# First loads of a fused attention and feed-forward block: q, k columns moved to another DMA queue, statistics of two tiles moved behind the first casts

## The chip, the cores and the metric

The kernel runs on one core of a Trainium2 chip. A core has five engines, each with its own instruction stream that runs in order: TensorE (PE, matrix products; its weight loads are listed as PEld), VectorE (DVE), ScalarE (ACT), GpSimd (POOL) and SyncE (SP), which here only starts transfers. Engines wait for each other through semaphores. Transfers are started by SP and by ScalarE, each with a queue of its own, and are carried out by 16 DMA engines. The metric is the device time of one execution in microseconds; lower is better.

## The reference

Inputs are in bf16: x is 1 x 2048 x 448, the hidden width of the feed-forward part is 1792.

```python
x = A_x
xn = _layernorm(x, axis=-1)
return x + _A_ref(xn, A_wqkv, A_wo) + _B_ref(xn, B_w_gate, B_w_up, B_w_down)

# _A_ref: 16 heads of 28, window of 256
qkv = (x @ wqkv).reshape(B, S, 3, H, Dh)           # then q, k, v
scores = einsum("bhqd,bhkd->bhqk", q, k) * Dh ** -0.5
mask = (i - j >= 0) & (i - j < 256)
o = einsum("bhqk,bhkd->bhqd", softmax(where(mask, scores, -1e9)), v)
return o.reshape(B, S, D) @ wo

# _B_ref
return (gelu(x @ w_gate) * (x @ w_up)) @ w_down
```

## The kernel before

The 2048 positions are 16 tiles of 128 and four blocks of 512. Everything is scheduled by hand: the order in which the Python code emits instructions is the order on each engine. A loop over the four blocks does attention and feed-forward of a block, and fills the time of the exponentials with matrix work of the neighbouring stages.

The part that the change touches comes before that loop and in its first steps.

Loads. SP starts x tile 0, x tiles 2 and 3, v's weights (rows 0 to 383, `wv`), the last 64 rows of q, k and v, x tiles 4 to 7, the remaining columns of q and k (`wraw`, L98), and then the first feed-forward weights. ScalarE starts x tile 1 and the first 4 heads' columns of q and k (L90).

Statistics. `stat(t)` (L155) takes mean and variance of tile t on DVE in two instructions (L157, L158). `rstd(t, n)` (L160) makes 1/sqrt(variance + 1e-5) from it, with a logarithm and an exponential on ACT (L166, L167), and for tile 5 alone with two instructions on POOL (L163, L164). `norm` (DVE, L176) or, for tile 1, `norm_scalar` (ACT, L184) applies it. For tiles 0 to 3 PE transposes the result (L199), and DVE or ACT copies it from PSUM to `xnT` (L200): DVE for tiles 0 and 3, ACT for 1 and 2. The transposes of tiles 0 and 2 use PSUM buffer b2, those of 1 and 3 use b3. Later tiles are transposed by DMA (`dma_transp`, L190).

First projections (L760 to L811). In PE's order: nine matmuls without use (`warmup`), transpose of tile 0, one more such matmul, transpose of tile 1, v of tile 0 (L776), transposes of tiles 2 and 3, v of tile 1, q and k of head group 0 (`proj`, L204), the last 64 rows of these (L210), v of tile 3. `pads` (L754) copies the q and k columns to a padded layout of 32 per head, first group 0 (q on DVE, k on ACT), then group 1, then 2 and 3. `qk_copies` casts q on ACT (L257) and k on DVE (L258) from PSUM; `v_copy` (L240) does so for v. On POOL, `make_masks` (L117) cuts the mask tiles, and `masked` (L619) applies the causal mask to the score blocks of steps 0 to 3, six instructions a step.

First block. For each step i of 8, scores are made on PE (L688), the exponential is taken on ACT (L693), and then the list `plan[i]` runs. `gen_qk` makes q and k of groups 1, 2 and 3 and is followed by `gen_up`, the up projection of the feed-forward part (L505, output `ue`). Their PSUM buffers are four (b0 to b3); `take` gives the one that has been free longest, `give` returns it at the end of the list. A group's q buffer is free once ACT has copied it, its k buffer once DVE has. The up projection's first pair uses the two buffers of group 2. `ahead2` (in `plan[1]`) takes statistics of tile 7 and normalises tiles 4 and 5, ahead of the cast of k of group 2; `ahead3` (in `plan[2]`) does tiles 6 and 7. The weighted sums of group 0 and 1 (`pv`, L662) come at steps 4 and 6 and read masked blocks of steps 0, 1 and 2, 3.

Of the kernel before, what the change touches and what calls it, by code (L numbers as in the profile page):

```python
# [16 lines left out]
S, D, H, Dh, F = 2048, 448, 16, 28, 1792  # L17
# [10 lines left out]
def kernel(  # L28
# [11 lines left out]
    nc = tc.nc  # L40
# [23 lines left out]
    wv = const.tile([P, 4, D], bf16, name="wv")  # L64
    v_sb = const.tile([P, NT, H, 32], bf16, name="v_sb")
    wraw = blk.tile([P, 4, 2 * D], bf16, name="wraw", tag="hT")
# [5 lines left out]
    def rows(w, c0, n):  # L72
        return w[c0 * P:(c0 + n) * P, :].rearrange("(c p) n -> p c n", p=P)
# [10 lines left out]
    wqk = rows(A_wqkv, 0, 3)[:, :, 0:2 * D]  # L84
    nc.sync.dma_start(out=x_sb[:, 0, :], in_=xv[:, 0, :])
    nc.vector.memset(x_sb[:, 1, 0:1], 0.0)
    nc.scalar.dma_start(out=x_sb[:, 1, :], in_=xv[:, 1, :])
    nc.sync.dma_start(out=x_sb[:, 2:4, :], in_=xv[:, 2:4, :])
    for c in (0, D):
        nc.scalar.dma_start(out=wraw[:, 0:3, c:c + 4 * Dh], in_=wqk[:, :, c:c + 4 * Dh])  # L90
    nc.sync.dma_start(out=wv[:, 0:3, :], in_=rows(A_wqkv, 0, 3)[:, :, 2 * D:3 * D])
    for a in range(2):
        nc.sync.dma_start(out=wraw[64 * a:64 * a + 64, 3, 0:D], in_=A_wqkv[384:448, a * D:(a + 1) * D])
    for a in range(2):
# [16 lines left out]
    def make_masks(n):  # L111
        for i, edges in list(enumerate(EDGES))[n]:
            for j, (_, *kinds) in enumerate(edges):
                for h, kind in enumerate(kinds):
                    if kind:
                        m = masks[64 * h:64 * h + 64, i, j, :]
                        nc.gpsimd.affine_select(out=m, in_=m, pattern=[[kind, 64]], compare_op=ALU.is_ge, fill=0.0,  # L117
                                                base=min(kind, 0), channel_multiplier=-kind)
# [36 lines left out]
    def stat(t):  # L155
        st = work.tile([P, nc.vector.BN_STATS_DIM], f32, name="st")
        nc.vector.bn_stats(out=st[:, :], in_=x_sb[:, t, :])  # L157
        nc.vector.bn_aggr(out=mv_all[:, t, :], in_=st[:, :])  # L158

    def rstd(t, n):  # L160
        lnv = work.tile([P, 4], f32, name="lnv")
        if t == 5:
            nc.gpsimd.tensor_scalar(out=lnv[:, 0:1], in0=mv_all[:, t:t + 1, 1], scalar1=1e-5, scalar2=None, op0=ALU.add)  # L163
            nc.gpsimd.tensor_tensor(out=rstd_all[:, t:t + 1], in0=lnv[:, 0:1], in1=minus_half[:, 0:1], op=ALU.pow)  # L164
            return
        nc.scalar.activation(out=lnv[:, 0:n], in_=mv_all[:, t:t + n, 1], func=ACT.Ln, bias=eps_t[:, 0:1], scale=1.0)  # L166
        nc.scalar.activation(out=rstd_all[:, t:t + n], in_=lnv[:, 0:n], func=ACT.Exp, scale=-0.5)  # L167
# [34 lines left out]
    def mm3(ps, lhs, rhs, start, stop):  # L202
        for c in range(3):
            nc.tensor.matmul(ps, lhsT=lhs(c), rhs=rhs(c), start=start and c == 0, stop=stop and c == 2,  # L204
                             skip_group_check=True)
# [27 lines left out]
    def v_dense(t, pv, first=True):  # L233
        mm3(pv, lambda c: xnT[:, c, t * P:(t + 1) * P], lambda c: wv[:, c, :], first, not first)
# [4 lines left out]
    def v_copy(t, pv, copy):  # L239
        copy(out=v_sb[:, t, :, 0:Dh], in_=pv.rearrange("p (h d) -> p h d", d=Dh))  # L240
        give(pv)
# [5 lines left out]
    def qk_halves(qb, g, pq, pk):  # L247
        w3 = w3p[:, 4 * g:4 * g + 4, :].rearrange("p h d -> p (h d)")
        for hi, ps in enumerate((pq, pk)):
            mm_half(ps, w3, xnT[:, 3, qb * QB:(qb + 1) * QB], hi, False, True)  # L250
# [73 lines left out]
    def deliver(qb):  # L324

        for j in range(4):
            nc.sync.dma_start(out=kT[32 * j:32 * j + Dh, 3, qb * QB:(qb + 1) * QB], in_=k3[j].rearrange("t i n -> (t i) n"))
# [149 lines left out]
    def new_hT(qb):  # L477
        hT = blk.tile([P, NF, QB], bf16, name="hT", tag="hT")
        hTs[qb] = hT
# [269 lines left out]
    def pads(eng, dst, gs):  # L749

        hs = slice(4 * gs.start, 4 * gs.stop)
        c0 = D * (dst is wkp)
        src = wraw[:, 0:3, c0 + Dh * hs.start:c0 + Dh * hs.stop]
        eng(out=dst[:, :, hs, 0:Dh], in_=src.rearrange("p c (h d) -> p c h d", d=Dh))  # L754
# [37 lines left out]
    nc.vector.tensor_copy(out=w3p[:, :, 0:Dh], in_=wraw[:, 3, 0:D].rearrange("p (h d) -> p h d", d=Dh))  # L792
    nc.vector.memset(masks[:, 0, 0, 0:1], 1.0)
    make_masks(slice(0, 1))
    stat(4)
    rstd(4, 1)
    stat(5)
    rstd(5, 1)
    make_masks(slice(1, 3))
    qk_halves(0, 0, pq, pk)  # L800
    for t in range(4):
        v_half(t, pvs[t], t < 2)
# [2 lines left out]
    v_copy(0, pvs[0], nc.scalar.copy)  # L805
    v_copy(1, pvs[1], nc.scalar.copy)
    pads(nc.vector.tensor_copy, wkp, slice(1, 2))
    v_dense(3, pvs[3], False)
    v_copy(3, pvs[3], nc.vector.tensor_copy)
    for dst in (wqp, wkp):  # L810
# [38 lines left out]
    for qb in range(NB):  # L849
        if qb in (1, 3):  # L850
            tc.mark_branch_hint_location("general", hint="LikelyTaken",
                                         engines=[mybir.EngineType.DVE if qb == 1 else mybir.EngineType.PE])
        early = ()
        if qb == 0:
            new_hT(0)
            early = (0, 1, 2, 3, 4)
            def last_v():
                v_dense(2, pvs[2], False)
                v_copy(2, pvs[2], nc.vector.tensor_copy)

            u = chain(gen_qk(), gen_up(0, (1, 2, 3, 0, 4), (2, 3, 4)))
            w = gen_pairs(1, (("v", 0), ("v", 2), ("k", 0), ("k", 1), ("k", 2)))
            plan = [[last_v, lambda: stat(6), (u, 3), ahead], [(u, 2), ahead2, (u, 2)], [(u, 1), ahead3, (u, 7)], [(u, 8), lambda: stat(8)],
                    [lambda: stat(9), (u, 12), lambda: fill_pads(True)], [(u, 9), "sums"],
                    [(w, 7), "inverse", "scale", (w, 7), lambda: stat(10), (w, 3)],
                    [(w, 4), lambda: stat(11), lambda: rstd(8, 4), (w, 7), "masks", "sums", (w, 7), "inverse"]]
        else:
            d = gen_down(qb - 1)
            if qb < 3:
                u = gen_pairs(qb + 1, (("v", 0), ("k", 0), ("v", 2), ("k", 1), ("k", 2)))  # L870
                plan = [[(d, 14)], [(d, 11)], [(d, 11)], [(u, 7)], [(d, 17)], ["sums", (d, 1), (u, 7), "inverse"], [(u, 11)],
                        [lambda: q_last(qb + 1, nc.vector.tensor_copy), (d, 6), "sums"], [(d, 2), "inverse", (d, 9)],
                        [(u, 9), "masks", (u, 1)]]
                plan[3] = [(d, 1), (u, 7)]
                if qb == 2:
                    plan[0], plan[2] = [(d, 13)], [(d, 10)]
                if qb == 1:
                    for i, j in enumerate((0, 1, 2, 2)):
                        plan[j].insert(0, lambda t=12 + i: stat(t))
                    plan[4].append(lambda: rstd(12, 4))  # L880
                    plan[1] = plan[1][:1] + [lambda: q_last(1, nc.vector.tensor_copy), (d, 8)]
                    plan[2] = plan[2][:2] + [(d, 12), lambda: collect(1)]
                    plan[4].append(lambda: deliver(1))
            else:
                new_hT(3)
                early = (1, 2, 3, 4, 5, 6)
                u = gen_up(3, early, (4, 5, 6))
                plan = [[(u, 12)], [(u, 9)], [(d, 12)], [(d, 10)], [(d, 12)], [(d, 1), (u, 7), "sums"], [(d, 12), "inverse"],
                        ["sums", "inverse", (d, 11)], [(d, 11)], [(d, 1), "masks", (u, 13), "masks", (u, 1)]]
        if qb in (1, 2):  # L890
            swap(qb + 1)
        score_pool(1)
        rest, after, flush = attention(qb, plan)
        nc.scalar.preload_act_table(ACT.Gelu_apprx_tanh)
        score_pool(2)
        if qb not in hTs:
            new_hT(qb)

        def hook(f):
            after(f)  # L900
            if qb in (1, 2) and f == 0:
                collect(qb + 1)
            if f == (8, 2, 2, 0)[qb]:
                o_collect(qb)
            if f == (12, 4, 4, 0)[qb]:
                o_deliver(qb)
                o_finish(qb)
            if qb == 0 and f == 10:
                nc.gpsimd.tensor_copy(out=wo[64:128, 3, :], in_=wo[0:64, 3, :])
            if qb in (1, 2) and f == 10:  # L910
                deliver(qb + 1)
            t = ({0: 8, 4: 9, 8: 10, 10: 11} if qb == 0 else {4: 12, 6: 13, 8: 14, 10: 15} if qb == 1 else {}).get(f)
            if t is not None:
                norm(t)
                dma_transp(t)
            if qb == 0 and f == 4:
                load_wo(3, 4)

        gated(qb, early, rest, flush, hook)
        if qb < NB - 1:  # L920
            nc.scalar.preload_act_table_set("natural_log_exp_and_others")
# [159 lines left out]
```

## Time and profile before

| | us |
|---|---|
| median of 3 runs | 211.65 (211.53 to 212.1) |
| span of the profiled execution | 210.4 |
| first matrix product that is part of the result (v of tile 0) | starts at 7.34 |
| last addition (L402) | 207.50 to 207.90 |

The profiled execution's span is from its first to its last instruction; the time of a run has some 1.25 us more around it (211.65 less 210.4). Times in the views are from the start of the span. A row of the timeline gives start, duration, engine and line, operation, output and inputs with their shapes, and how often; in brackets stands the idle time of the engine before it and what ended that. SPq and ACTq rows are the issues of transfers, not the transfers. The chain of work that ended last is short in this profile (the last addition and what follows it), so the path is read from the timeline of each engine.

### The profile page before, as it was taken

To read this page: it belongs to the slowest core of one execution; us is meant where nothing else is said; L and a number is where in the kernel's file an instruction comes from. 1 tells how busy PE (TensorE), PEld (TensorE's weight loads), DVE (VectorE), ACT (ScalarE), POOL (GpSimd) and SP (SyncE) were. 2 spreads that over 40 slices of the span, in tenths; PEclk is the share of its full clock that TensorE was granted. 3 is DMA by queue.
4 is the path that set the end of the run, shared out by engine and by line. 5 is a ranking of instruction groups with operands and counts; after the bars stand their busy time and mean duration, and the time that the engine had idled before them with its cause. 6 is when DMAs were issued, how large, how long until landed. Compare 5 with 4: busy or idle time off the path is not lost. (4 is left out here: it accounts for less than half of the span.)

```text
span 210.4 us, 6677 instructions
## 1 busy us (share of the span) xinstructions
PE 205.3 (98%) x2842; PEld 98.4 (47%) x2842; DVE 156.6 (74%) x360; ACT 134.5 (64%) x132; POOL 44.3 (21%) x89
## 2 busy tenths in 40 slices
PE   7899999999999999999999999999999999999994
PEld 2443444544454545444445444544444454544572
DVE  6798989899788985696438897395385699596532
ACT  4689896956677977413778788523587787756000
POOL 5289932241000220040000112013000022032000
PEclk9999999999999999999999999999999999999999
DMA  5999599973341001003331000100000010100011
GB/s 171 277 244 207 112 207 224 296 237 82 74 103 53 25 11 31 9 3 72 71 75 47 25 3 24 23 3 21 22 5 0 3 47 3 45 9 16 3 47 50
DMA packets 24890, 15.68 MB, mean 75 GB/s; under 512 B 9208, under 2 KB 24728, under 8 KB 24856
## 3 DMA queue, kind: packets, MB, share of 16 engines
q1 hardware_dynamic: 23912, 14.93, 30.2%
q8 instruction: 23, 0.38, 0.7%
q10 hardware_dynamic: 944, 0.29, 0.6%
q14 instruction: 11, 0.09, 0.2%
HBM read 9.26 MB, written 2.41 MB: 55 GB/s over the span
## 5 line engine op out<-in xcount | busy, mean ns | idle before, releaser
L693 ACT ACTIVATE p_sb<-sc 128x2048 bf16<-128x2048 f32 x38 | 71.4, 1879 | 16.9 <-PE sc L688 11.7
L545 ACT ACTIVATE p_sb<-gt 128x1024 bf16<-128x1024 f32 x28 | 28.6, 1025 | 31.3 <-PE gt L505 30.4
L628 POOL TENSOR_TENSOR oN<-oc,l 128x512 bf16<-128x512 f32 x16 | 20.7, 1298 | 120.5 <-DVE l L641 120.5
L505 PE MATMUL gt<-xnT,wg 64*128 64x512 bf16 x224 | 45.6, 376 | 0.0
L414 PE MATMUL po<-wd,hT 128*128 128x448 bf16 (+1 forms) x224 | 44.7, 347 | 0.0
L505 PE MATMUL gt<-xsw,wg 64*128 64x512 bf16 x168 | 40.7, 376 | 0.0
L613 DVE TENSOR_TENSOR p_sb<-p_sb,masks 128x256 bf16<-128x256 bf16 (+1 forms) x98 | 30.9, 369 | 7.4 <-ACT p_sb L693 7.4
L555 DVE TENSOR_TENSOR hT<-p_sb,u 128x512 bf16<-128x512 bf16 x34 | 21.8, 675 | 13.5 <-PE u L505 13.5
L414 PEld LDWEIGHTS <-hT 128*128 128x128 bf16 x238 | 21.9, 98 | 19.1 <-issue 2.2
L505 PEld LDWEIGHTS <-wg 64*128 64x128 bf16 x392 | 19.0, 94 | 22.3
L505 PEld LDWEIGHTS <-wu 64*128 64x128 bf16 x392 | 18.7, 94 | 22.2 <-issue 0.4
L505 PE MATMUL u<-xnT,wu 64*128 64x512 bf16 x136 | 28.1, 376 | 0.0
L505 PE MATMUL u<-xsw,wu 64*128 64x512 bf16 x102 | 24.7, 376 | 0.0
L505 PE MATMUL ue<-xnT,wu 64*128 64x512 bf16 x88 | 18.0, 377 | 0.0
L647 DVE TENSOR_TENSOR oc<-oc,ov 128x512 f32<-128x512 f32 (+1 forms) x16 | 10.4, 656 | 10.0 <-ACT oc L645 9.9
L505 PE MATMUL ue<-xsw,wu 64*128 64x512 bf16 x66 | 16.3, 377 | 0.0
L688 PE MATMUL sc<-qT,kT 28*64 28x320 bf16 (+4 forms) x736 | 16.2, 259 | 0.0
L402 DVE TENSOR_TENSOR res<-po,x_sb 128x448 bf16<-128x448 f32 (+1 forms) x14 | 8.1, 605 | 7.8 <-PE po L414 6.7
L688 PEld LDWEIGHTS <-kT 28*64 28x64 bf16 x736 | 8.1, 103 | 12.3 <-issue 11.0
L522 DVE CAST hT<-ue 128x512 bf16<-128x512 f32 x16 | 10.5, 685 | 2.7 <-PE ue L505 2.7
L645 ACT COPY oc<-ov 128x512 f32<-128x512 f32 x16 | 9.3, 585 | 4.0 <-PE ov L662 4.0
L641 DVE STREAM_TRANSPOSE l<-inv_all 128x512 f32<-128x512 f32 x16 | 11.1, 701 | 0.1
(115 smaller groups left out, 257.0 us busy)
## 6 DMA issues: line engine op xcount, KB each, us to landing
out_dram<-res SPq DMA_DIRECT2D x15, 112.0 KB
wd<-in_B_w_down_dram SPq DMA_DIRECT2D x2, 784.0 KB
x_sb<-in_A_x_dram SPq DMA_DIRECT2D x3, 448.0 KB
xsw<-xnT SPq DMA_DIRECT2D x6, 192.0 KB
wg<-in_B_w_gate_dram SPq DMA_DIRECT2D x2, 560.0 KB
wu<-in_B_w_up_dram SPq DMA_DIRECT2D x4, 224.0 KB
wu<-in_B_w_up_dram SPq DMA_DIRECT2D x2, 336.0 KB
wraw<-in_A_wqkv_dram SPq DMA_DIRECT2D x2, 252.0 KB
```

The source lines that it names most:

```text
L414: nc.tensor.matmul(po[:, 0:w], lhsT=x[:, k, tt * P:(tt + 1) * P], rhs=wt[:, k, lo:up], start=start and n == 0, stop=stop and n == len(term ...
L505: nc.tensor.matmul(ps, lhsT=w[64 * hi:64 * hi + 64, c, p * P:(p + 1) * P], rhs=xchunk(qb, hi, c, qb * QB, QB), start=c == 0, stop=c == 6, ...
L522: copy(out=hTs[qb][:, p + 7 * i, :], in_=us[i])
L545: nc.scalar.activation(out=ges[p][:, :, :], in_=gt[:, :, :], func=ACT.Gelu_apprx_tanh)
L555: nc.vector.tensor_tensor(out=hT[:, p + 7 * i, :], in0=ge[:, i, :], in1=u, op=ALU.mult)
L613: nc.vector.tensor_tensor(out=reg, in0=reg, in1=m, op=ALU.mult)
L628: nc.gpsimd.tensor_tensor(out=oN[:, g, :], in0=oc[:, :], in1=inv, op=ALU.mult)
L641: nc.vector.transpose(out=l1[:, :, :], in_=inv_all[:, 4 * qb + g, :].unsqueeze(2).to_broadcast([P, 16, 32]))
L645: nc.scalar.copy(out=oc[:, :], in_=ov[0][:, :])
L647: nc.vector.tensor_tensor(out=oc[:, q0:], in0=oc[:, q0:], in1=ov[1][:, q0:], op=ALU.add)
L688: nc.tensor.matmul(ss[k0:k0 + nk, j, col:col + nq], lhsT=kT[r, g, kt * P + k0:kt * P + k0 + nk], rhs=qT[r, g, ring(qb).start + q0:ring(qb) ...
L693: nc.scalar.activation(out=p_sb[:, :, 0:ncol], in_=ss[:, :, 0:ncol], func=ACT.Exp, scale=SCALE)
```

## The change

Three parts. The loads of the first 4 heads' q and k columns go from ScalarE's queue to SP's, behind the load of v's weights; ScalarE's queue keeps x tile 1 alone. The statistics of tiles 4 and 5, tile 5's rstd on POOL and the second and third mask tiles go from ahead of the last rows of q, k of group 0 to behind the casts of group 0 and the padded copies of group 1. Tile 4's rstd on ACT goes into the plan of the first attention step.

```diff
     nc.scalar.dma_start(out=x_sb[:, 1, :], in_=xv[:, 1, :])
     nc.sync.dma_start(out=x_sb[:, 2:4, :], in_=xv[:, 2:4, :])
+    nc.sync.dma_start(out=wv[:, 0:3, :], in_=rows(A_wqkv, 0, 3)[:, :, 2 * D:3 * D])
     for c in (0, D):
-        nc.scalar.dma_start(out=wraw[:, 0:3, c:c + 4 * Dh], in_=wqk[:, :, c:c + 4 * Dh])
-    nc.sync.dma_start(out=wv[:, 0:3, :], in_=rows(A_wqkv, 0, 3)[:, :, 2 * D:3 * D])
+        nc.sync.dma_start(out=wraw[:, 0:3, c:c + 4 * Dh], in_=wqk[:, :, c:c + 4 * Dh])
     for a in range(2):
...
     make_masks(slice(0, 1))
-    stat(4)
-    rstd(4, 1)
-    stat(5)
-    rstd(5, 1)
-    make_masks(slice(1, 3))
     qk_halves(0, 0, pq, pk)
     for t in range(4):
         v_half(t, pvs[t], t < 2)
     qk_copies(0, 0, pq, pk)
     pads(nc.vector.tensor_copy, wqp, slice(1, 2))
     v_copy(0, pvs[0], nc.scalar.copy)
     v_copy(1, pvs[1], nc.scalar.copy)
     pads(nc.vector.tensor_copy, wkp, slice(1, 2))
+    stat(4)
+    stat(5)
+    rstd(5, 1)
+    make_masks(slice(1, 3))
     v_dense(3, pvs[3], False)
     v_copy(3, pvs[3], nc.vector.tensor_copy)
...
-            plan = [[last_v, lambda: stat(6), (u, 3), ahead], [(u, 2), ahead2, (u, 2)], [(u, 1), ahead3, (u, 7)], [(u, 8), lambda: stat(8)],
+            plan = [[last_v, lambda: rstd(4, 1), lambda: stat(6), (u, 3), ahead], [(u, 2), ahead2, (u, 2)], [(u, 1), ahead3, (u, 7)], [(u, 8), lambda: stat(8)],
```

## The prediction

> **What bounds the kernel now.** I read the page first, then busy time in stretches of 5 us.
>
> ```profile
> span 210.4 us, 6677 instructions
> ...
> PE 205.3 (98%) x2842; PEld 98.4 (47%) x2842; DVE 156.6 (74%) x360; ACT 134.5 (64%) x132; POOL 44.3 (21%) x89
> ```
> ```profile
> 10.00:15.00 5.00, 5.00 (x64) 1.88 (x63) 4.69 (x13) 4.27 (x7) 4.14 (x17) 1.00 1.09 248
> 15.00:20.00 5.00, 5.00 (x52) 1.84 (x58) 4.97 (x13) 4.97 (x7) 4.66 (x14) 1.00 1.21 240
> ```
>
> In the second fence each row gives the stretch, its length, then busy us and instructions of PE, PEld, DVE, ACT and POOL, the granted clock and the DMA share. PE has no idle left from 10 us on; the end is where PE's stream starts plus its length. So the change is worth what it moves that stream, early on, less any new hole in it. VectorE (DVE) and ScalarE (ACT) are full too between 15 and 20 us: 4.97 of 5. That stretch has no room for more work. The clock is 1.00 throughout.
>
> The hole at the start, in the timeline of PE alone (start, duration, instruction, idle time before it):
>
> ```profile
> 6.30 0.40 PE L199 MATMUL tp<-ident,xn 128*128 128x128 bf16 x4
> 7.34 0.73 PE L204 MATMUL pv<-wv,xnT 128*128 128x448 bf16 x3 [0.65 <-DMA wv<-in_A_wqkv_dram]
> 7.91 0.61 PE L199 MATMUL tp<-ident,xn 128*128 128x128 bf16 x8
> ```
>
> PE waits 0.65 us for v's weights. Everything behind stands in line: the transposes of x tiles 2 and 3, then the projections.
>
> **The loads.** In the DMA view of 3.2 to 7.3 us (packets, MB, share of 16 engines) SP's queue is q1, and ScalarE's, q10, holds only the first q, k columns:
>
> ```profile
> q1 hardware_dynamic: 1110, 0.91, 76.6%
> q10 hardware_dynamic: 800, 0.17, 20.4%
> ```
> ```profile
> 1.48 0.99 ACTq L90 DMA_DIRECT2D wraw<-in_A_wqkv_dram  x2
> ```
>
> They take 20.4% of 4.1 us = 0.84 us of each engine, in the very time in which v's weights travel. Behind them on one queue they leave that 0.84 to the weights: landing 7.34 - 0.84 = 6.50. The bounds: no gain at all (7.34), or all of it. I take nearly all, since the packets of the two queues stand in the same stretch.
>
> A rule of the Trainium skill, page "DMA: Bandwidth & Descriptors", section "Issuing engines are not separate DMA queues", speaks against this: transfers from any engine run on the same 16 engines and interleave, and a second issuer saves only its issue time. Read strictly it makes the move worth nothing and the time 212.6; that is rival 2. The 20.4% above counts against it, since order within a queue is what changes.
>
> SP issues two more DMAs, 0.99 us by ACT's row. Its later loads, tiles 4 to 7 among them, are issued that much later, but the engines are still at work on what was issued before, so landing follows the bytes, which are the same. SP also waits for these columns, in its timeline:
>
> ```profile
> 5.78 2.08 SPq L98 DMA_DIRECT2D wraw<-in_A_wqkv_dram  x2
> ```
>
> The two issues of the remaining q, k columns, some 0.4 us of work each, are stretched over 2.08 us because each waits until the first columns of its half have landed, the k half at about 7.5. Landing of the k columns at 6.50 + 0.84 = 7.34 leaves that as it is. On ACT 0.99 us of issue time goes, before an activation that waits for DVE's statistics anyway: worth nothing.
>
> **How much earlier PE gets.** The views of DVE and of ACT (one row):
>
> ```profile
> 6.19 0.39 DVE L200 COPY xnT<-tp 128x512 bf16<-128x512 bf16 x1
> 6.70 0.81 DVE L176 TENSOR_SCALAR xn<-x_sb,mv_all,rstd_all 128x448 bf16<-128x448 bf16 x2
> 7.43 0.27 DVE L754 COPY wqp<-wraw 128x336 bf16<-128x336 bf16 x1
> 8.55 0.42 DVE L200 COPY xnT<-tp 128x512 bf16<-128x512 bf16 x1 [0.86 <-PE tp L199]
> ...
> 9.21 0.63 DVE L157 BATCH_NORM_STATS2 st<-x_sb 128x6 f32<-128x448 bf16 x1
> ...
> 10.60 0.18 DVE L158 BATCH_NORM_AGGREGATE mv_all<-st 128x2 f32<-128x6 f32 x1
> 10.90 0.69 DVE L258 CAST kT<-s 128x512 bf16<-128x512 f32 x1
> ...
> 11.69 0.26 DVE L754 COPY wkp<-wraw 128x336 bf16<-128x336 bf16 x1
> 11.92 0.62 DVE L240 CAST v_sb<-pv 128x448 bf16<-128x448 f32 x1
> ...
> 14.29 0.18 DVE L158 BATCH_NORM_AGGREGATE mv_all<-st 128x2 f32<-128x6 f32 x1
> 14.59 0.69 DVE L258 CAST kT<-pk 128x512 bf16<-128x512 f32 x1
> ...
> 17.45 0.68 DVE L258 CAST kT<-pk 128x512 bf16<-128x512 f32 x1
> ...
> 19.43 0.68 DVE L258 CAST kT<-pk 128x512 bf16<-128x512 f32 x1
> 20.70 0.69 DVE L522 CAST hT<-ue 128x512 bf16<-128x512 f32 x1 [0.59 <-PE ue L505]
> ```
> ```profile
> 6.99 0.57 ACT L200 COPY xnT<-tp 128x512 bf16<-128x512 bf16 x1
> ```
>
> Tile 0's activations are copied at 6.58, so the first v projection could start at 6.65. The transposes of tile 3 follow in PE's order, but they write the PSUM buffer that ACT's copy of tile 1 frees at 6.99 + 0.57 = 7.56, whatever the loads do. Four transposes take 0.40 (row of 6.30): tile 3's copy starts at 7.56 + 0.05 + 0.40 = 8.01 in place of 8.55. So the head gains at most 0.53, call it d, and all up to the first casts (L257, L258) moves with it. DVE must have copied the first q columns by 8.01, so they must land by 7.74; half of 0.84 behind 6.50 puts them at 6.92. If in one line they went at the pace of the other packets (q1: 76.6% of 4.1 us on 16 engines for 1110 packets, 45 ns each; 24 packets per engine) they would land at 7.58: still in time. I take d = 0.45, some hand-offs below the bound; d runs from 0 to 0.53.
>
> **The statistics.** The pair of tiles 4 and 5 costs DVE 10.60 + 0.18 - 9.21 = 1.57 us, about 1.5 as instructions overlap a little at their ends. Today it lies in front of the cast at 10.90, which waits for PE and not for DVE (free at 10.78). With PE earlier by d it would stand in the way; so it goes behind the casts. But what it leaves is a hole in DVE from about 8.7 to 10.4, and where it goes DVE is full: from 10.90 to 20.1 it has only one wait, at 14.59 for PE (it was free at 14.47, and could have begun at about 14.40: 0.17). So every DVE instruction behind it comes at -d + 1.5, from the cast of group 1 at -d + 1.33.
>
> Who waits for that? PSUM buffers pass round. Of the q, k buffers of group 2, the first that the feed-forward's up projection takes needs ACT's copy, the second the cast of 17.45 to 18.13. PE takes them here:
>
> ```profile
> 18.53 0.38 PE L505 MATMUL ue<-xsw,wu 64*128 64x512 bf16 x1
> ```
>
> Slack today: 18.53 - 18.13 - 0.05 = 0.35. Ahead, the buffers of the v copies and the padded weights of groups 2 and 3 have slack of 0.2 or more by the same sum and hold. So PE stops there until 18.13 + 1.33 - d + 0.05, and goes on later than today by 1.33 - 0.35 - d = 0.98 - d. With d = 0.45: **+0.53 us**. Behind it PE is again the slower one (DVE's 0.59 of idle time at 20.70), so the delay stays to the end; nothing later gives it back, since PE is full.
>
> GpSimd (POOL) says the same by another road. Tile 5's rstd (L163) stands in its order ahead of the masks and the masked score blocks:
>
> ```profile
> 11.49 0.31 POOL L163 TENSOR_SCALAR lnv<-mv_all 128x1 f32<-128x1 f32 x1
> ...
> 24.58 2.64 POOL L619 TENSOR_SCALAR_AFFINE_SELECT p_sb<-p_sb 64x256 bf16<-64x256 bf16 x6
> ```
> ```profile
> 28.11 0.62 PE L662 MATMUL ov<-p_sb,v_sb 64*32 64x320 bf16 x36
> ```
>
> It now waits for the statistics, 11.92 - 0.45 + 1.57 + 0.05 = 13.09, 1.6 later. POOL has no wait from there to 27.2, so the last masked block ends at 27.22 + 1.6 = 28.8. The weighted sum of group 1 uses that block in its second half, from about 28.35 today: +0.5 as well. Two roads to the same size make the lag more likely, and removing one alone would not remove it.
>
> The rstd of tile 4 moves on ACT behind the first exponential:
>
> ```profile
> 16.81 0.30 ACT L166 ACTIVATE lnv<-mv_all,eps_t 128x2 f32<-128x2 f32 x1
> 17.14 0.20 ACT L167 ACTIVATE rstd_all<-lnv 128x2 f32<-128x2 f32 x1
> ```
>
> Its 0.50 us delays the copy of q of group 1, by some 0.2 net, and the second exponential by as much; PE meanwhile has d in hand, so at most 0.1 shows, inside the lag above and not added to it. Without that cover it would cost up to 0.5.
>
> **Sum.** Span 210.4 + 0.53 = 210.9; the median of the runs, 211.65, lies 1.25 above the span, so 212.2.
>
> **Rivals.** 1, the forecast: 212.2, from 211.9 (d = 0.53 and a lag 0.15 shorter) to 212.6; chance 0.63. 2, v's weights land no earlier: d = 0, 0.98 of lag: 212.6. For it: the engines are near full, and the skew between them may set the landing. Against: the 20.4%. Chance 0.13. 3, not slower: DVE's lag does not reach PE and d stays to the end: 211.65 - 0.5 = 211.15. It decides at the up projection's second matmul: the group 2 cast must end by 18.53 - d - 0.05, and POOL's last block must not bind, so both lags must shrink by about 1 us. For it: only my reading of the buffers' round and of two queues' order says otherwise. Against: two full engines. Chance 0.14. 4, the first q columns come late in one line: each 0.1 after 7.74 takes 0.1 from d. With both halves at 45 ns ahead of DVE's copy, 6.50 + 2.16 = 8.66, tile 3's copy starts at 8.93, d = -0.4: 211.65 + 1.4 = 213.0. For it: such short packets (0.17 MB in 800) are not seen in one line with the others. Against: the 0.8 us to spare at the pace that q10 shows. Chance 0.10.
>
> **Numbers.** A measurement here can tell about 0.3% = 0.63 us from no change: above 212.28 or below 211.02. Slower: half of rival 1, and 2 and 4: 0.53. Faster: the better part of rival 3: 0.09. Within: 0.38. Range 211.3 to 212.9: it reaches rival 2 whole, most of 4 and up to 3.
>
> **What would show it.** Right: the first v matmul at about 6.7 with no DMA wait, tile 3's copy at about 8.05, DVE idle up to 10.4, the cast of group 2 ending near 19.0, an idle stretch of about 1 us on PE at the up projection with DVE as releaser, POOL's L163 near 13.1. Wrong: the first v matmul still at 7.3 (rival 2), no PE idle near 18 to 19 (rival 3), DVE waiting for wraw at the first padded copy (rival 4).

## The result and the profile after

| | before | after |
|---|---|---|
| median of 13 runs each, same chip, us | 211.65 (211.45 to 212.74) | 213.05 (212.61 to 215.05) |
| ratio, with 95% interval | | 1.0068 (1.0049 to 1.0088) |
| span of the profiled execution | 210.4 | 211.1 |

The change makes the kernel slower by 1.4 us; 212.2 was forecast, with a range that ended at 212.9. The page of the profile after, and its busy time by stretch (us from the start, length, then busy us and instructions of PE, PEld, DVE, ACT and POOL, granted clock, DMA share, GB/s):

```profile
span 211.1 us, 6677 instructions
...
PE 205.2 (97%) x2842; PEld 98.1 (46%) x2842; DVE 155.9 (74%) x360; ACT 134.4 (64%) x132; POOL 43.9 (21%) x89
```
```profile
5.50:8.00 2.50, 1.79 (x17) 1.15 (x18) 2.00 (x7) 2.35 (x7) 0.00 (x0) 1.00 0.54 126
...
15.00:20.00 5.00, 4.55 (x42) 1.59 (x39) 4.93 (x14) 4.32 (x6) 4.44 (x16) 1.00 1.17 255
```

PE does the same work in the same time. Between 15 and 20 us it now has 0.45 us of idle time where it had none, and between 5.5 and 8 us the DMA engines are half idle. The same stretch of before:

```profile
5.50:8.00 2.50, 1.85 (x14) 0.92 (x13) 2.03 (x7) 1.99 (x6) 0.00 (x0) 1.00 1.00 271
```

PE's timeline of after, at the three places that count (start, duration, engine and line, operation, count, and in brackets the idle time before it):

```profile
6.55 0.74 PE L204 MATMUL pv<-wv,xnT 128*128 128x448 bf16 x3
...
18.01 0.37 PE L505 MATMUL ue<-xnT,wu 64*128 64x512 bf16 x1
18.83 0.39 PE L505 MATMUL ue<-xsw,wu 64*128 64x512 bf16 x2 [0.45 <-DVE kT L258]
...
28.41 0.54 PE L662 MATMUL ov<-p_sb,v_sb 64*32 64x320 bf16 x20
29.11 0.35 PE L662 MATMUL ov<-p_sb,v_sb 64*32 64x320 bf16 x16 [0.17 <-POOL p_sb L619]
```

The wait for v's weights is gone (6.55 against 7.34). At the up projection PE stands still for the cast of group 2 and is 0.30 late (18.83 against 18.53). At the weighted sum of group 1 it waits for POOL's masked block: the two halves of that sum were 28.11 and 28.35 before, 0.24 apart; now they are 0.70 apart, and the second is 0.76 late. The span ends 0.72 later. So these two places, 0.30 at the first and 0.46 (0.70 less 0.24) at the second, account for the difference between the two profiles. DVE and POOL in their timelines:

```profile
7.34 0.27 DVE L754 COPY wqp<-wraw 128x336 bf16<-128x336 bf16 x1
7.94 0.42 DVE L200 COPY xnT<-tp 128x512 bf16<-128x512 bf16 x1 [0.33 <-PE tp L199]
...
10.28 0.69 DVE L258 CAST kT<-s 128x512 bf16<-128x512 f32 x1 [1.72 <-PE s L210]
10.89 0.27 DVE L754 COPY wqp<-wraw 128x336 bf16<-128x336 bf16 x1
11.47 0.28 DVE L754 COPY wkp<-wraw 128x336 bf16<-128x336 bf16 x1 [0.32 <-DMA wraw<-in_A_wqkv_dram]
11.66 0.61 DVE L157 BATCH_NORM_STATS2 st<-x_sb 128x6 f32<-128x448 bf16 x1
...
16.84 1.36 DVE L176 TENSOR_SCALAR xn<-x_sb,mv_all,rstd_all 128x448 bf16<-128x448 bf16 x4
18.10 0.68 DVE L258 CAST kT<-pk 128x512 bf16<-128x512 f32 x1
```
```profile
13.38 0.23 POOL L163 TENSOR_SCALAR lnv<-mv_all 128x1 f32<-128x1 f32 x1 [2.59 <-DVE mv_all L158]
...
26.70 2.36 POOL L619 TENSOR_SCALAR_AFFINE_SELECT p_sb<-p_sb 64x256 bf16<-64x256 bf16 x6
```

DVE is idle for 1.72 us ahead of its cast at 10.28: the hole that the statistics left. Then comes a wait that the forecast did not have: 0.32 us for the remaining k columns, straight ahead of the statistics. POOL waits 2.59 us for these and ends its last masked block at 26.70 + 2.36 = 29.06, just before PE's second half starts.

SP's queue after, and what its small loads weigh (KB each in the DMA view):

```profile
2.23 1.02 SPq L91 DMA_DIRECT2D wraw<-in_A_wqkv_dram  x2
3.29 1.21 SPq L93 DMA_DIRECT2D wraw<-in_A_wqkv_dram  x2
4.55 1.24 SPq L95 DMA_DIRECT2D wv<-in_A_wqkv_dram  x2
5.83 0.58 SPq L96 DMA_DIRECT2D x_sb<-in_A_x_dram  x1
6.46 1.04 SPq L98 DMA_DIRECT2D wraw<-in_A_wqkv_dram  x2
```
```profile
wraw<-in_A_wqkv_dram SPq DMA_DIRECT2D x2, 56.0 KB
wv<-in_A_wqkv_dram SPq DMA_DIRECT2D x2, 56.0 KB
```

The four loads of last rows (L93, L95) cost SP some 0.6 us each to issue and carry 56 KB, which at 271 GB/s is 0.21 us. From 3.29 to 5.79 SP issues only these. What lay ahead of them is used up by about 5.5, and tiles 4 to 7 (L96) and the remaining columns (L98) are issued only then. The events of these loads' semaphores in the traces agree: tiles 4 to 7 have landed at 9.58, at 9.18 before, and the remaining k columns at 11.44, at 10.74 before. With two issues less ahead of it on this queue, the issue of tiles 4 to 7 stood 1.06 us earlier before the change:

```profile
4.77 0.59 SPq L96 DMA_DIRECT2D x_sb<-in_A_x_dram  x1
```

### The profile page after: what moved, and what is told of

Read it like the earlier page. It is cut to its first block, busy times and chain, and to the rows that moved or that the text cites. A ratio compares the mean times of both kernels' runs of the same rounds, so it can differ in the third digit from the quotient of the medians.

```text
span 211.1 us, 6677 instructions
## 1 busy us (share of the span) xinstructions
PE 205.2 (97%) x2842; PEld 98.1 (46%) x2842; DVE 155.9 (74%) x360; ACT 134.4 (64%) x132; POOL 43.9 (21%) x89
## 5 line engine op out<-in xcount | busy, mean ns | idle before, releaser
L613 DVE TENSOR_TENSOR p_sb<-p_sb,masks 128x256 bf16<-128x256 bf16 (+1 forms) x98 | 30.4, 364 | 7.6 <-ACT p_sb L693 7.6
L662 PE MATMUL ov<-p_sb,v_sb 64*32 64x320 bf16 (+4 forms) x720 | 11.0, 253 | 0.2 <-POOL p_sb L619 0.2
```

What stands on the lines that cost most here:

```text
L613: nc.vector.tensor_tensor(out=reg, in0=reg, in1=m, op=ALU.mult)
L662: nc.tensor.matmul(ov[half][32 * j:32 * j + 32, q0:q0 + nq], lhsT=v_sb[r, kt, 4 * g + j, :], rhs=p_sb[r, j, col:col + nq], start=n == half ...
```

## The experiments

Two questions: which part costs what, and by which road; and why the measured 1.4 is more than the 0.53 of the forecast. The theory: the moved statistics cost by DVE and by POOL, the moved loads cost because SP's later loads come late, and the first profile of before was of an execution slower than its median. The rivals: that one part alone makes all of the loss; that POOL's road or DVE's alone is the bound; that the 1.25 us around the span holds. Ratios are against runs of the kernel before that were taken together with each (medians 211.68 to 211.81).

**The kernel before, again.** No edit.

> The kernel before, unchanged, for more executions and a second profile. Theory A (the profile that the forecast rests on was a slow execution, 0.4 us above the median run): spans of the median run near 209.95 us, so that run time less span is about 1.7 us and not 1.25; first v matmul of this profile at 6.7 to 7.1 us instead of 7.34. Rival B (the moved loads themselves cost more than was counted): the profile looks as the first one did, v at 7.3, span 210.4 at a median of 211.65.

211.68, ratio 0.9998 (0.9989 to 1.0007). Its profiled execution has a span of 210.1 in a run of 211.80, 1.7 apart, and so are run and span in the other runs, to within 0.2 (for the profiled one of after: 212.79 and 211.1). A median of 211.65 goes with a span near 209.95, and the profile that the prediction rests on was 0.4 above that. In PE's timeline the hole is smaller: v's first matmul starts 0.25 earlier than in the first profile, and the span ends 0.28 earlier (210.08 for 210.36). The row names a DVE instruction that ended just then, but the load of v's weights has landed only at 7.05 by its semaphore:

```profile
6.28 0.40 PE L199 MATMUL tp<-ident,xn 128*128 128x128 bf16 x4 [0.23 <-ACT xn L184]
7.09 0.73 PE L204 MATMUL pv<-wv,xnT 128*128 128x448 bf16 x3 [0.42 <-DVE xn L176]
```

**The loads alone.**

```diff
+    nc.sync.dma_start(out=wv[:, 0:3, :], in_=rows(A_wqkv, 0, 3)[:, :, 2 * D:3 * D])
     for c in (0, D):
-        nc.scalar.dma_start(out=wraw[:, 0:3, c:c + 4 * Dh], in_=wqk[:, :, c:c + 4 * Dh])
-    nc.sync.dma_start(out=wv[:, 0:3, :], in_=rows(A_wqkv, 0, 3)[:, :, 2 * D:3 * D])
+        nc.sync.dma_start(out=wraw[:, 0:3, c:c + 4 * Dh], in_=wqk[:, :, c:c + 4 * Dh])
```

> Only the loads move; the statistics of tiles 4 and 5 stay ahead of the first casts. These wait for tiles 4 to 7, which landed at about 9.6 us in the changed kernel, so the cast of k is not before 11.15 us (10.90 before). Theory A: 0 to +0.5 us against before (211.6 to 212.1). Rival B: the later landing of everything on SP's queue is most of the 1.4 us: +1.0 us or more (212.6).

212.21, ratio 1.0018 (1.0009 to 1.0027): the loads alone cost 0.5 by the medians, 0.4 by the ratio. DVE in the timeline:

```profile
9.79 0.63 DVE L157 BATCH_NORM_STATS2 st<-x_sb 128x6 f32<-128x448 bf16 x1 [1.17 <-DMA x_sb<-in_A_x_dram]
...
11.28 0.66 DVE L258 CAST kT<-s 128x512 bf16<-128x512 f32 x1
```

v's first matmul is at 6.62, but tile 4 is not there when DVE wants it (its load lands at 9.77 by its semaphore), and the statistics hold up the cast of group 0, 0.64 behind its 10.64 in the second profile of before. With the loads moved and the statistics left in place, it is these that wait for x.

**The statistics alone.** `stat(4)`, `stat(5)`, `rstd(5, 1)` and the masks behind the first casts and tile 4's rstd in the plan as in the change, the loads as before.

> Only the statistics move; the loads stay as before. Theory A with the forecast's sum at d = 0: +1.0 us (212.6), PE idle at the up projection's second matmul and again at the weighted sum of group 1 (waiting for POOL). Rival B: at most +0.4 us (212.0).

212.70 (212.56 to 213.01), ratio 1.0043 (1.003 to 1.0056): +1.0. In POOL's and PE's timelines of this kernel:

```profile
13.27 0.23 POOL L163 TENSOR_SCALAR lnv<-mv_all 128x1 f32<-128x1 f32 x1 [2.32 <-DVE mv_all L158]
```
```profile
28.54 0.53 PE L662 MATMUL ov<-p_sb,v_sb 64*32 64x320 bf16 x20
29.33 0.34 PE L662 MATMUL ov<-p_sb,v_sb 64*32 64x320 bf16 x16 [0.26 <-POOL p_sb L619]
```

POOL waits as in the kernel after, and PE waits for it. The wait at the up projection that was expected is not marked in this profile: its second matmul is at 18.45, 0.18 behind the 18.27 of the second profile of before. So here POOL's road sets the end almost alone. This is the larger part of the loss, and the moved loads have no share in it.

**POOL's road taken away, with the loads moved.**

```diff
     stat(4)
     stat(5)
+    make_masks(slice(1, 3))
     rstd(5, 1)
-    make_masks(slice(1, 3))
```

> The changed kernel with the second and third mask tiles ahead of tile 5's rstd on POOL, so that POOL works while it waited 2.6 us. If POOL's road sets the end (0.73 us late at the weighted sum of group 1, 0.30 at the up projection): 0.4 us less than the changed kernel, 212.6, and no wait for POOL at the weighted sum. If DVE's road alone sets it: no difference, 213.05.

212.44, ratio 1.0042 (1.0025 to 1.0059): 0.6 less than the kernel after. POOL's row, then PE's:

```profile
14.22 0.23 POOL L163 TENSOR_SCALAR lnv<-mv_all 128x1 f32<-128x1 f32 x1
```
```profile
18.73 0.39 PE L505 MATMUL ue<-xsw,wu 64*128 64x512 bf16 x2 [0.41 <-DVE kT L258]
```

POOL has no wait left, since it makes the masks while DVE does the statistics; PE still stops at the up projection. Each road costs by itself. How the 0.6 is made up is less sure: the k columns landed at 11.23 in this profile and DVE copied them at 11.25, 0.22 earlier than in the kernel after, though the loads are the same.

**The same, with the loads as before.**

> Loads as before, statistics behind the first casts, the mask tiles ahead of tile 5's rstd on POOL: DVE's road alone. Two roads (theory): POOL's part, 0.6 us, falls away from the 1.0 us of the kernel with the statistics alone: 212.05 to 212.2, PE idle only at the up projection. If POOL's wait was all of it: 211.7, as before.

212.43, ratio 1.0037 (1.0024 to 1.005): DVE's road alone costs 0.7, more than was expected here. The up projection's second matmul is at 18.77, 0.50 behind the 18.27 of the second profile of before.

**The loads moved, x tiles 4 to 7 issued sooner; the statistics as before.**

```diff
+    nc.sync.dma_start(out=x_sb[:, 4:8, :], in_=xv[:, 4:8, :])
     for a in range(2):
         nc.sync.dma_start(out=wraw[64 * a:64 * a + 64, 3, 0:D], in_=A_wqkv[384:448, a * D:(a + 1) * D])
     for a in range(2):
         nc.sync.dma_start(out=wv[64 * a:64 * a + 64, 3, :], in_=A_wqkv[384:448, 2 * D:3 * D])
-    nc.sync.dma_start(out=x_sb[:, 4:8, :], in_=xv[:, 4:8, :])
```

> Loads moved, statistics ahead of the casts as before, and x tiles 4 to 7 issued ahead of the last 64 rows of q, k and v. If the 0.45 us that the loads alone cost come from SP's issues, which bring tiles 4 to 7 0.6 us later and hold the statistics up, this removes them: tiles land by 9.0, cast of k at 10.4 to 10.5, 0.1 to 0.3 us faster than before (211.4 to 211.6). If the late columns or rows of q and k cost it: 212.0 or more.

211.76, ratio 1.0001 (0.9992 to 1.001): the 0.5 of the loads is gone. In the busy time by stretch and in SP's timeline:

```profile
5.50:8.00 2.50, 2.12 (x21) 1.19 (x19) 2.06 (x7) 2.34 (x7) 0.00 (x0) 1.00 1.01 271
```
```profile
3.30 0.49 SPq L92 DMA_DIRECT2D x_sb<-in_A_x_dram  x1
```

The issues are as many as in the kernel after, on the same queue and for the same bytes, but one of 448 KB now stands ahead of the four small ones, and the engines are full: 271 GB/s in place of 126. Tiles 4 to 7 have landed at 8.20 in place of 9.77. So it was the order that starved the engines: small loads at 0.6 us an issue with nothing large behind which to hide. There is no gain over before, though v's first matmul is at 6.67: now the last rows of q, k come late (DVE waited 0.20 for them at 8.68), and the cast of k, expected at 10.4 to 10.5, is at 10.79.

**One pair ahead, one behind.** `stat(4)` stays ahead of group 0's last rows, `stat(5)`, the masks and then `rstd(5, 1)` go behind, in the order of the kernel with POOL's road taken away; loads as in the change.

> Changed loads and their order, mask tiles first on POOL, statistics of tile 4 ahead of the casts and of tile 5 behind. DVE's lag shrinks by 0.75 us, below what PE has to spare, so no idle PE at the up projection: 211.5 to 211.8. If the lag is set by something else than the inserted statistics: 212.4, as with the mask tiles first alone.

211.98, ratio 1.0017 (1.0007 to 1.0028), somewhat above what was expected. DVE's row:

```profile
9.97 0.63 DVE L157 BATCH_NORM_STATS2 st<-x_sb 128x6 f32<-128x448 bf16 x1 [1.12 <-DMA x_sb<-in_A_x_dram]
```

The pair ahead waits 1.12 us for x, so the place is free but what it needs isn't there.

**The split, and tiles 4 to 7 sooner.**

> Loads moved, tiles 4 to 7 ahead of the last rows, mask tiles first on POOL, statistics of tile 4 ahead of the casts and of tile 5 behind. If late tiles and late q, k columns were what kept the split of the statistics from paying (cast of k at 10.73 instead of 10.3, 0.34 us of DVE waiting for the columns): cast of k at 10.3 to 10.4, cast of group 2 done by 17.9, no idle PE at the up projection, its second matmul at about 18.0, span 209.8, time 211.4 to 211.5. If DVE is still the bound there: 211.8 or more.

211.60 (211.41 to 212.23), ratio 1.0001 (0.9992 to 1.0011). In PE's timeline there is no wait left at the up projection:

```profile
17.93 0.38 PE L505 MATMUL ue<-xnT,wu 64*128 64x512 bf16 x1
17.93 0.59 PE L505 MATMUL ue<-xsw,wu 64*128 64x512 bf16 x2
```

Its profiled span, 209.7, is the shortest of all, but spans of before also reach 209.7, and the medians differ by less than 0.1. It is no better than before as far as can be told.

**Two more orders of SP's loads**, tiles 4 to 7 between the last rows of q, k and those of v: with the split, and with both statistics ahead.

> As the kernel before this one, but tiles 4 to 7 between the last rows of q, k and those of v, so that the copy of these rows does not hold DVE up. Same account: 211.4 to 211.5, a little below the kernel with the tiles first if the copy at 8.68 us was late; the same otherwise; 211.8 or more if DVE is still the bound at the up projection.

212.90 (211.77 to 213.67), ratio 1.0054 (1.0037 to 1.007). The profiled run took 211.77 and shows nothing amiss. Why most others took 1.1 us more is open.

> Loads moved, tiles 4 to 7 between the last rows of q, k and those of v, both statistics ahead of the casts as before. DVE ends them at about 10.6, so the cast of k comes at 10.6 against 10.79 with the tiles first: 211.5 to 211.6. If tiles land later than 9.2 in this order: 211.8.

211.80 (211.53 to 213.16), ratio 1.0016 (1.0 to 1.0033): no gain here either, and again a tail of long runs.

**The kernel after, again.** No edit.

> The changed kernel again, for a second profile. By the account so far its end is the start of the up projection's second matmul plus 191.8 us plus what POOL adds at the weighted sum of group 1: matmul at 18.7 to 18.9, POOL 0.4 to 0.8, run time 1.7 above the span, 212.6 to 213.3. If the median of 213.05 has another cause, the span is above 211.5 with the same two numbers.

213.28 (212.59 to 213.75), ratio 1.0072 (1.0054 to 1.009); span 211.5. In DVE's timeline the wait for the k columns has grown:

```profile
11.88 0.28 DVE L754 COPY wkp<-wraw 128x336 bf16<-128x336 bf16 x1 [0.60 <-DMA wraw<-in_A_wqkv_dram]
```

Against the first profile of after this copy is 0.41 later (11.88 for 11.47), the second half of the weighted sum 0.43 (29.54 for 29.11), and the end of the span 0.4. Of the 0.41, 0.28 is this wait and 0.12 the cast in front of it (10.40 for 10.28); what comes late here goes through to the end. The up projection's second matmul is at 19.25, later than the expected 18.7 to 18.9, but the sum holds: 19.25 + 191.8, and 0.47 that POOL adds, make the span of 211.5.

**The kernel after without that wait in the way.**

```diff
+    stat(4)
+    stat(5)
     pads(nc.vector.tensor_copy, wkp, slice(1, 2))
-    stat(4)
-    stat(5)
     rstd(5, 1)
```

> The changed kernel with both statistics ahead of the padded copy of k's columns of group 1, which waited 0.32 and 0.60 us for its load in the two profiles. If the late columns are the third part of the cost: DVE and POOL's L163 0.3 to 0.6 us earlier (about 13.1), the weighted sum of group 1 and the end with them, 212.5 to 212.8. If the wait was hidden: 213.05 or more, as the copy then comes 1.5 us later and PE waits for it at the projection of k of group 1.

212.41 (212.26 to 212.63), ratio 1.003 (1.0019 to 1.0042): 0.64 less than the kernel after, and the spread over 7 runs is 0.4 us, against 2.4 over 13 (212.61 to 215.05). DVE's and POOL's rows:

```profile
12.66 0.24 DVE L754 COPY wkp<-wraw 128x336 bf16<-128x336 bf16 x1
```
```profile
12.91 0.23 POOL L163 TENSOR_SCALAR lnv<-mv_all 128x1 f32<-128x1 f32 x1 [2.00 <-DVE wkp L754]
```

The copy no longer waits and POOL's rstd comes 0.47 earlier. (Its row names the copy, which DVE ends at 12.90, behind the statistics.) The 0.6 that stays goes by this account with the moved statistics.

## Why the prediction was wrong

The direction and both roads of the delay were right: slower, through DVE at the up projection and through POOL at group 1's weighted sum. The time was too low by 0.85 us, and three terms make that up: 0.45 for what lies around the span, 0.19 between the profiles, 0.27 by which the median execution of after lies above its profiled one. (They sum to 0.91; 210.36 + 0.53 + 1.25 is 212.14, which the forecast gave as 212.2.) So two steps failed: the first term is a wrong sum over two executions, and the other two go back, as far as is shown, to one wrong step about the loads, "landing follows the bytes".

**The first step that failed: "the median of the runs, 211.65, lies 1.25 above the span, so 212.2".** The span of 210.4 and the median belong to different executions. Within one execution the run lies 1.7 above the span, so the sum's 210.9 meant a run of 212.6, and the profiled execution, by the same 1.7, was one of 212.1, like the slowest of the three runs shown. That execution already had a loss in its head, which the change then seemed to win back: 0.25 us against the second profile of before (7.34 for 7.09), and by the spans 0.4 against the median execution.

**The gain d of the head**, 0.45, was sized on the same execution. Against it, it came true: first v matmul with no DMA wait at 6.55 ("about 6.7"), tile 3's copy at 7.94 ("about 8.05"), first q columns in time for DVE's copy at 7.34. Rival 4 falls; that its 213.0 is the number measured is chance. But the four profiles with the old loads have v's first matmul at 7.34, 7.09, 6.88 and 6.74, mean 7.01; the ten with the new loads at 6.55 to 6.83, mean 6.68. The hole of 0.65 us was the largest of the four, and the mean gain at this matmul is 0.33. Less of it gets through: v of tile 1 (the next L204 row) starts at 8.35, 8.10, 7.89 and 7.81 with the old loads, mean 8.04, and at a mean of 7.85 with the new, 0.19 sooner. Among the kernels with the statistics behind the casts, the cast of k of group 0 comes at 10.43 and 10.35 with the old loads and at 10.28 to 10.40 with the new, so that hardly any gain is left there.

The rule of the Trainium skill weighed in the prediction ("DMA: Bandwidth & Descriptors", "Issuing engines are not separate DMA queues"), read strictly as it was there, does not hold for v's weights. By the events of its semaphore this load has landed at 6.70 to 7.30 in the four profiles with the old loads (mean 6.97) and at 5.41 to 6.43 in the ten with the new (mean 6.00). That is 0.97 sooner, about the 0.84 of the prediction, so rival 2 falls, and PE gains less because it then waits for something else (in the profile of after for ACT's normalisation of tile 1, until 6.21). The rule's other half, that a second issuer saves issue time, is what the prediction took too lightly: the section calls that time usually small relative to the DMA, and here an issue took 0.6 us for bytes that at 271 GB/s need 0.21.

**The second step that failed: "landing follows the bytes, which are the same".** This held only while a backlog hid SP's issues. The share fell to 0.54, tiles 4 to 7 landed at 9.55 to 9.95 in the six profiles with the loads as in the change and at 8.64 to 9.18 in the four with the old loads, and in the two profiles of after the k columns came 0.32 and 0.60 us after DVE wanted them. Through POOL's L163, 13.38 where 13.09 was forecast, it put the last masked block at 29.06 in place of 28.8. That is where the profiles come to differ by 0.72 and not by 0.53, 0.19 more. The last 0.27 (213.05 - 1.7 = 211.35, less the profiled 211.08) fits it too: the second profile of after shows the wait larger and the span 0.4 longer. That it is this wait in the runs without a trace is argued from the narrow spread of the last experiment, not seen.

**DVE's road: right, a size off.** The forecast had the cast of group 2 end at 19.0 and PE stop until 19.06; it was 18.10 + 0.68 = 18.78, and 18.83. The row of four normalisations in front of it (L176) took 1.36, in the kernel before 1.59 (last section). The cast thus began 0.23 sooner than the 18.33 that the forecast's terms give (17.45 + 1.33 - 0.45): 0.23 by this row, 0.17 by the head (cast of group 0 at 10.28, not 10.45), 0.32 the other way by the k columns, and 0.15 of small gaps that were not followed up. PE was late by 0.30 in place of 0.53 there; the rest came by POOL.

**"Two roads to the same size … removing one alone would not remove it": half right.** With POOL's road removed the loss is 0.73 (212.44 - 211.71) and not 1.4, so removing one takes off about half; with the loads as before it takes off 0.27 (212.70 - 212.43). The roads are not two names for one delay: POOL's binds 10 us later and adds what it is longer by. No experiment took DVE's road alone away, but in the kernel with the statistics alone it cost only 0.18 at the up projection (18.45 for 18.27), and the loss was 1.0 all the same.

**Tile 4's rstd on ACT**, at most 0.1 and hidden: among PE's waits after 10 us none names ACT, which agrees; it was not tried alone. It took 0.28 and 0.20 us there (at 13.51 and 13.83), close to the 0.50 that the prediction read from rows of two other tiles.

By parts, against before: loads alone +0.5, statistics alone +1.0, both +1.4. What the loads cost depends on what waits for them: 0.35 on top of the statistics (213.05 less 212.70), nothing with the masks first (212.44 with the loads moved, 212.43 without).

## What to carry to other kernels

Tie a profile to a run before subtracting from it: compare its span with the spans of several runs, and where a hole is to be filled, see whether it is there in a second profile. When transfers move to another queue, add up the issue time of all that stands behind them, and look for small loads in a row: put a large one ahead of them. Work that leaves a hole in one engine for a place where that engine is full pays at each engine that waits for it in order, so follow every consumer to the end, a slow one such as POOL first.

## What the hardware showed that was not expected

DVE's normalisation (bf16 to bf16, from SBUF to SBUF) has no fixed price. By operation and shape (busy us, mean ns), between 15 and 18.3 us, first in the kernel with the statistics alone, then in the one with the masks made first:

```profile
L176 DVE TENSOR_SCALAR xn<-x_sb,mv_all,rstd_all 128x448 bf16<-128x448 bf16 x2 | 0.8, 379 | 0.0
L176 DVE TENSOR_SCALAR xn<-x_sb,mv_all,rstd_all 128x64 bf16<-128x64 bf16 x2 | 0.6, 290 | 0.0
```
```profile
L176 DVE TENSOR_SCALAR xn<-x_sb,mv_all,rstd_all 128x448 bf16<-128x448 bf16 x2 | 1.0, 480 | 0.0
L176 DVE TENSOR_SCALAR xn<-x_sb,mv_all,rstd_all 128x64 bf16<-128x64 bf16 x2 | 0.8, 384 | 0.0
```

In the first POOL is at its small masks at that time (64x64, L117, from 14.19 to 17.75), in the second at the wide ones:

```profile
15.07 7.39 POOL L619 TENSOR_SCALAR_AFFINE_SELECT p_sb<-p_sb 64x256 bf16<-64x256 bf16 x18
```

The group of four in DVE's timeline, in the kernel with the statistics alone and then in the kernel before:

```profile
16.72 1.09 DVE L176 TENSOR_SCALAR xn<-x_sb,mv_all,rstd_all 128x448 bf16<-128x448 bf16 x4
```
```profile
15.95 1.59 DVE L176 TENSOR_SCALAR xn<-x_sb,mv_all,rstd_all 128x448 bf16<-128x448 bf16 x4
```

In the ten profiles in which POOL is at the wide masks all the while, the group took 1.37 to 1.71 us; the 1.09 is the only group with POOL at the small masks nearly to its end. With POOL going over to the wide masks in the middle of the group it took 1.36 in both profiles of after (at 17.74 in the first) and 1.24 in the last experiment. So the 0.5 us of the first row goes together with what POOL does, in one profile; the 0.23 of the kernel after lies at the edge of what the group takes anyway. The cause was not tried.
